# A pooled attention with a mixture of attention experts: five engine queues ordered anew, K pooling in wider matmuls, gates by counting, and another split of the last two output chunks

## The chip, the cores and the metric

The kernel runs on one core of one Trainium2 chip. The metric is device time in microseconds (us) of one execution, as the median of several runs. The profile is taken of one execution; its span runs from the first to the last instruction.

The engines have short names. PE is TensorE (matmuls; its weight loads are listed as PEld), DVE is VectorE, ACT is ScalarE, POOL is GpSimd, SP is SyncE. Each engine works through its own queue strictly in order. POOL also issues the input loads, SP the output stores.

## The reference

Two stages follow one another. Shapes: batch 8, heads 8, sequence 576, head size 64, so a token has 512 features; 4 experts with a head size of 64, of which each token uses 2.

```python
# stage 1: attention over keys and values averaged in groups of 8
k_p = k.reshape(B, H, S // 8, 8, D).mean(axis=3)      # 72 pooled keys
v_p = v.reshape(B, H, S // 8, 8, D).mean(axis=3)
attn = softmax(q @ k_p.T / sqrt(D))
x = (attn @ v_p)  # -> (B, S, H * D)
# stage 2: per token the two best of four experts, each a causal attention
logits = x @ w_gate
w = softmax over the top 2 logits of each token
for e in range(4):
    a = causal_softmax((x @ wq[e]) @ (x @ wk[e]).T / sqrt(Hd))
    ye = a @ (x @ wv[e]) @ wo[e]
    out += (e is in the token's top 2) * w * ye
```

## The kernel before, in words

Everything is unrolled. The work of a batch is cut into small steps, and the order of all steps of all eight batches is written out by hand in one long string, SEQ (lines 632 to 702). The loop below it reads the string token by token and emits the instructions of each step. A token is a name, arguments, a colon, the batch, and for matmul steps `@` and the PSUM bank; a trailing `d` puts a copy on DVE and not on ACT, a trailing `p` leaves a store to a later token. `tc.manual_schedule` keeps every engine's instructions in the order of the string, and only adds the waits that the data need. So the string fixes five queues at once, and where a token stands against one of another engine has no effect beyond those waits.

The steps of one batch, with their names in the string:

- Loads (`L`, line 112, on POOL): k and v in three thirds each, q in four quarters. They land in three rotating raw buffers each (NRAW = 3, line 55), cast to bf16 on the way. A load can start when the batch three before it has been read out.
- Pooling of k and v as matmuls with a pooling matrix: `PK` (line 265) and `PV` (line 284). For each third and each of two token parities, `PK` issues four matmuls on 32-wide strips of the array, 24 of 128 columns for a whole batch; batch 0 (LONG, line 59) is done in two halves of 64 columns. DVE turns the result (`kc`), a copy casts it (`kt`), another copies the pooled v (`vc`).
- DVE transposes q in two halves (`u0`, `u1`; line 293).
- Stage 1: scores `E`, exponential `e` on ACT, sums `D` and `d`, reciprocals `x`, weighted values `O`, and the scaled result `o` (DVE) into xT.
- Stage 2: values and gate logits `V`, `v`; query and key projections `P`, `p`; scores `S`, exponentials `s` (ACT, line 490), causal masks `a` (POOL, line 508), and the weighted values `B` with their scaling `bz`, `bg`, `b` (DVE, line 549).
- The gate `g0` to `g9` (line 397): an exponential on ACT, and eleven small DVE instructions that find the second largest of four logits by maxima and minima, compare, and normalize.
- The result is transposed on PE (`T`, copied by `t`) or by a DMA on SP (`F`, line 584). Then comes the output projection `Y` (line 592), its copy `y` (line 602) and the store `z` (line 617; `zs` on SP).

A batch's 576 tokens are four chunks of 128 and a tail of 64; the tails of two neighbouring batches share one chunk, number 4. In `Y`, the last chunk of all (batch 7, chunk 4) is computed in two halves of 256 columns in two banks. Tokens `ya` and `yb` copy the halves on ACT and DVE, and its two stores of 64 tokens go out on SP and ACT.

The exponential of the 64-token tile (`s` with tile number 3) is two ACT instructions, one for each expert of a pair:

```python
if ti == 3:
    for e in range(2):
        nc.scalar.activation(out=et[half(b), :, e, eo : eo + n], ...)
```

Of the kernel before, what the change touches and what calls it, by code (L numbers as in the profile page):

```python
# [16 lines left out]
ISEQ = mybir.AluOpType.is_equal  # L17
EXP = mybir.ActivationFunctionType.Exp
# [3 lines left out]
def kernel(  # L22
# [12 lines left out]
    nc = tc.nc  # L35
# [24 lines left out]
    HALF = TPP // 2  # L60

# [325 lines left out]
    def small(b, nm, *shape):  # L387
        if (b // 2, nm) not in at:
            at[b // 2, nm] = gtp.tile([128, NPC, *shape], FP32, name=nm, tag=nm)
        return at[b // 2, nm]  # L390
# [6 lines left out]
    def gate(b, step):  # L397
# [14 lines left out]
        elif step == 1:  # L412
            L2 = L.rearrange("p c (a b) -> p c a b", b=2)
            for nm, op in (("hi", MAXOP), ("lo", MINOP)):
                nc.vector.tensor_tensor(
                    out=tmp(nm, 2, 1), in0=L2[:, :, :, 0:1], in1=L2[:, :, :, 1:2], op=op
                )
        elif step == 2:
            for nm, src, op in (("s2", "hi", MINOP), ("s3", "lo", MAXOP)):
                nc.vector.tensor_tensor(  # L420
                    out=tmp(nm, 1), in0=got(src)[:, :, 0, :], in1=got(src)[:, :, 1, :], op=op
                )
        elif step == 3:
            nc.vector.tensor_tensor(
                out=tmp("m2", 1), in0=got("s2"), in1=got("s3"), op=MAXOP
            )
        elif step == 4:
            nc.vector.tensor_tensor(
                out=tmp("msk", E), in0=L, in1=got("m2").to_broadcast([128, n, E]), op=ISGE
            )  # L430
        elif step == 5:
            nc.vector.tensor_mul(out=tmp("W", E), in0=got("Ex"), in1=got("msk"))
        elif step == 6:
# [3 lines left out]
        elif step == 7:  # L437
# [4 lines left out]
        elif step == 8:  # L442
# [47 lines left out]
    def sb(b, bank, dve, ep, ti):  # L490
# [4 lines left out]
        if ti == 3:  # L495
            for e in range(2):
                nc.scalar.activation(
                    out=et[half(b), :, e, eo : eo + n],
                    in_=psum[half(b), bank + e, 0 : 2 * n].rearrange("p (a n) -> p a n", a=NEP),
                    func=EXP, scale=MOE_EXP_SCALE,  # L500
                )
# [90 lines left out]
    def Y(b, bank, c):  # L592
        p0 = 128 * place(b, c)
        last = (b, c) == (B - 1, 4)
# [7 lines left out]
    def y(b, bank, dve, c, half=None, later=False):  # L602
        ofin = at[b, "ofin", c] if (b, "ofin", c) in at else ofp.tile([128, DM], FP32, name="ofin", tag="ofin")
        if half is not None:
            cols = slice(256 * half, 256 * half + 256)
            copy(half == 1, ofin[:, cols], psum[:, bank ^ half, cols])
            at[b, "ofin", c] = ofin
            if (b, "half", c) not in at:
                at[b, "half", c] = True
                return  # L610
        else:
            copy(dve, ofin[:], psum[:, bank, :])
        at[b, "ofin", c] = ofin
        if not later:
            z(b, c, nc.sync)

    def z(b, c, queue):
        ofin = at[b, "ofin", c]
        if c == 4:
            for h in range(2):  # L620
                (nc.scalar if h and b == B - 1 else queue).dma_start(
                    out=out[b - 1 + h, MAIN:S, :], in_=ofin[64 * h : 64 * h + 64, :]
                )
# [12 lines left out]
        H1:0@0c H1:0@0c L_q1:1 H1:0@0c e21:0 e20:0 e11:0 D2:0@4 D0:0@5 L_q2:1 PV:0@6 d0:0 D1:0@7 vc:0d H1:0@0 x0:0  # L636
        c0:0d L_q3:1 d2:0 O00:0@6 d1:0 c1:0d O20:0@5 O01:0@4 o00:0 O10:0@2 x1:0 O11:0@3 o01:0 x2:0 X0:0@0 W2:0 o10:0
        X1:0 o11:0 X2:0 W3:0 c2:0d X3:0 c3:0d o20:0 P_k0:0@4 L_v0:1 h0:0 P_t0:0@5 p_k0:0d L_v1:1 P_k1:0@3 p_t0:0 L_v2:1
# [3 lines left out]
        d1:1 g1:0 E2:1@06 D0:1@2 vc:1d a03:0 x1:1 H1:0@3 L_v1:2 e20:1 g2:0 O11:1@3 e21:1 g3:0 O10:1@4 d0:1 o11:1 D2:1@5  # L642
        O01:1@6 L_v2:2 S10:0@0 x0:1 o10:1 S12:0@2 d2:1 s10:0 o01:1 S11:0@4 O00:1@7 g4:0 PK:2@6 s11:0 o00:1 L_k0:3
        O20:1@0 B01:0@1 kc:2 x2:1 B00:0@7 L_k1:3 g0:0 P_q1:1@4 o20:1 kt:2 bz00:0 bz01:0 s12:0 g5:0 L_k2:3 V2:1@0 g6:0
        g7:0 P_q0:1@6 g8:0 L_q0:3 v2:1 u1:2 p_q1:1 P_t0:1@0 a11:0 u0:2 p_q0:1 E1:2@24 L_q1:3 p_t0:1 g9:0 P_k0:1@6
        bg00:0 a10:0 e10:2 b00:0 bg01:0 L_q2:3 b01:0 V0:1@7 e11:2 p_k0:1d a12:0 E0:2@02 v0:1d B10:0@6 L_q3:3 W4:0 e01:2
        V4:1@4 bz10:0 B11:0@7 bg10:0 L_v0:3 b10:0 e00:2 PV:2@5 v4:1d D1:2@6 bz11:0 L_v1:3 P_k1:1@4 vc:2d d1:2 bg11:0
        b11:0 x1:2 E2:2@02 L_v2:3 D0:2@6 p_k1:1d e21:2 O11:2@7 O01:2@5 d0:2 O00:2@2 o11:2 O10:2@4 L_k0:4 e20:2 PK:3@3
        x0:2 o10:2 S03:1@0 S10:1@6 L_k1:4 s03:1 o01:2 s10:1 S01:1@0 o00:2 L_k2:4 V3:1@4 s01:1 kc:3 V1:1@5 L_q0:4 v3:1d
        S02:1@6 S11:1@2 v1:1 kt:3d S12:1@0 s02:1 L_q1:4 V2:2@4 u1:3 P_q1:2@5 a03:1 u0:3 s11:1 L_q2:4 P_q0:2@6 v2:2d  # L650
        s12:1 a02:1 p_q1:2d S00:1@2 L_q3:4 p_q0:2d g0:1 E0:3@04 s00:1 g1:1 L_v0:4 P_k0:2@6 g2:1 e00:3 g3:1 a12:1 g4:1
        P_k1:2@7 p_k0:2d e01:3 L_v1:4 E2:3@02 g5:1 B12:0@6 g6:1 L_v2:4 g7:1 e20:3 B02:0@4 g8:1 e21:3 bz12:0 T10:0@5
        g9:1 p_k1:2 a10:1 E1:3@02 bg12:0 t10:0d L_k0:5 b12:0 bz02:0 B12:1@5 bg02:0 e11:3 b02:0 PK:4@6 L_k1:5 bz12:1
        bg12:1 PV:3@4 b12:1 e10:3 kc:4 S00:2@2 L_k2:5 D1:3@5 vc:3d B01:1@6 s00:2 L_q0:5 kt:4d B02:1@7 T00:0@4 bz01:1
        V1:2@0 d1:3 bz02:1 L_q1:5 bg01:1 bg02:1 T02:0@1 t00:0d T01:0@2 D2:3@3 x1:3 b02:1 D0:3@5 a11:1 b01:1 O10:3@4
        d2:3 O00:3@7 t01:0d d0:3 L_q2:5 D2:2@6 v1:2d T11:0@3 V0:2@2 t02:0 o10:3 x0:3 a01:1 T12:0@5 V3:2@1 u0:4 L_q3:5
        t12:0 v0:2 O20:2@4 O01:3@5 v3:2 O11:3@0 a00:1 o00:3 t11:0 d2:2 L_v0:5 PV:4@1 o11:3 x2:2 x2:3 E0:4@26 o01:3 vc:4
        a00:2 Y3:0@0 L_v1:5 e01:4 o20:2 P_q1:3@5 y3:0dp e00:4 L_v2:5 T12:1@4 u1:4 B10:1@1 P_k1:3@0 p_q1:3 t12:1d bz10:1
        L_k0:6 bg10:1 E1:4@26 b10:1 p_k1:3 g1:2 P_t0:2@5 L_k1:6 e11:4 g2:2 V0:3@4 p_t0:2d Y2:0@0 e10:4 v0:3d Y1:0@5
        y2:0dp L_k2:6 V2:3@4 y1:0p g3:2 E2:4@26 O20:3@0 L_q0:6 v2:3d D1:4@1 e21:4 D0:4@5 o20:3 e20:4 PK:5@4 d1:4 L_q1:6  # L660
        u0:5 S02:2@2 d0:4 S10:2@6 V4:3@1 kc:5 s02:2 B11:1@5 kt:5d P_k0:3@4 v4:3 g4:2 bz11:1 a02:2 s10:2 bg11:1 b11:1
# [128 lines left out]
```

## Time and profile before

| what | value |
|---|---|
| median of 3 runs | 154.63 us (154.28 to 155.75) |
| span of the profiled execution | 152.5 us |
| granted PE clock, mean | 0.997 |
| data moved by DMA | 26.67 MB |
| input loads (queue of POOL) | 14.72 MB |
| DMA transposes on SP | 16 |

The time of the profiled execution itself isn't listed apart from the runs; its span is 2.1 us under their median. How to read the page: the busy shares say how long each engine had an instruction in work. The slices show the same over time, in tenths, for 40 equal slices of 3.8 us. The chain follows the work that ended last back to its causes. A group row gives the line, engine and operation, the shapes, the count, then busy time and mean length, then the idle time ahead of it and who ended it. A timeline row begins with the start and the length. In the windows, each engine's busy time in a stretch is followed by its number of instructions, and the row ends with the granted clock, the DMA share and the GB/s. An issue row of the DMA ends with the time from issue to landing.

### The profile page before, as it was taken

What the parts mean: (1) busy time and instruction counts of PE and PEld (TensorE: products, weight loads), DVE (VectorE), ACT (ScalarE), POOL (GpSimd) and SP (SyncE); (2) the same over time, 40 slices, a digit from 0 to 9 for tenths busy, and PEclk for the clock granted to TensorE, in tenths of its full rate; (3) what the DMA queues carried; (4) which work ended last, traced back from release to release, by engine and by line L of the source; (5) the groups of instructions that cost most, each with busy time, mean ns of one, the idle gap of its engine ahead of it and who ended that gap; (6) DMA issues with size and microseconds to landing.
All of it is one profiled execution on the core that took longest, in us unless ns stands there. A gap on an engine that the chain in (4) does not pass through costs nothing.

```text
span 152.5 us, 5419 instructions
## 1 busy us (share of the span) xinstructions
PE 140.5 (92%) x2101; PEld 78.8 (52%) x2122; DVE 125.9 (83%) x415; ACT 135.1 (89%) x247; POOL 89.5 (59%) x161
## 2 busy tenths in 40 slices
PE   6776998999999999999999999999999999999970
PEld 2323353465554465565546655856356667546640
DVE  1784846899899899899989999999897699888960
ACT  3359479999999999999999999999999899999860
POOL 6998588999688979958998171123300344442300
PEclk9999999999999999999999999999999999999998
DMA  4999999999999999999999931536528241389994
GB/s 126 237 186 181 181 179 178 180 180 181 179 188 180 179 181 182 178 180 182 169 173 176 181 34 39 211 84 208 176 92 325 83 121 25 66 282 306 333 340 134
DMA packets 68890, 26.67 MB, mean 175 GB/s; under 512 B 62720, under 2 KB 64000, under 8 KB 68864
## 3 DMA queue, kind: packets, MB, share of 16 engines
q0 software_dynamic: 57408, 14.72, 97.2%
q1 hardware_dynamic: 11088, 10.88, 22.2%
q10 hardware_dynamic: 368, 0.72, 1.5%
q8 instruction: 16, 0.26, 0.6%
q14 instruction: 10, 0.08, 0.2%
HBM read 30.42 MB, written 9.44 MB: 261 GB/s over the span
## 4 chain that ended last, share of the span: by engine, by line
PE 66%; DVE 11%; DMA 10%; POOL 4%; ACT 3%; issue 2%; DVEq 0%; POOLq 0%
PE psum L221 65%; DMA qraw<-in_q_dram 5%; DMA wst_q<-in_moe_wq_dram 4%; DVE xT L377 4%; ACT etb L503 2%; POOL kraw L126 2%; POOL vraw L126 2%; PE psum L230 1%; DVE qT L298 1%; DVE osc L562 1%; DVE oT L212 1%; POOL qraw L126 1%; DVE vp L212 1%; DVE ofin L212 1%; ACT eta L331 1%
## 5 line engine op out<-in xcount | busy, mean ns | idle before, releaser
L503 ACT ACTIVATE etb<-psum 128x1024 bf16<-128x1024 f32 x48 | 47.2, 1032 | 0.8 <-PE psum L221 0.4
L520 POOL TENSOR_SCALAR_AFFINE_SELECT etb<-etb 128x256 bf16<-128x256 bf16 x64 | 25.7, 412 | 37.2 <-ACT etb L503 36.0
L331 ACT ACTIVATE eta<-psum 96x1024 bf16<-96x1024 f32 (+1 forms) x48 | 36.0, 802 | 1.1 <-PE psum L221 0.4
L221 PEld LDWEIGHTS <-etb 128*128 128x128 bf16 x480 | 18.0, 97 | 6.3 <-issue 3.5
L126 POOL DMA_DIRECT2D qraw<-in_q_dram x30 | 19.7, 662 | 2.5 <-DVE gt L557 0.8
L377 DVE TENSOR_TENSOR xT<-psum,rza 128x512 bf16<-128x512 f32 x32 | 20.2, 681 | 1.0 <-ACT rza L354 0.5
L221 PE MATMUL psum<-wvg,xT 128*128 128x260 bf16 x144 | 20.8, 275 | 0.1
L126 POOL DMA_DIRECT2D kraw<-in_k_dram x25 | 19.0, 765 | 2.3 <-POOLq L774 0.8
L221 PE MATMUL psum<-vaug,etb 128*128 128x65 bf16 x480 | 20.2, 193 | 0.0
L126 POOL DMA_DIRECT2D vraw<-in_v_dram x24 | 18.8, 785 | 2.3 <-PE psum L221 1.4
L221 PE MATMUL psum<-xT,wqp 128*128 128x64 bf16 (+1 forms) x123 | 19.2, 282 | 0.5 <-issue 0.2
L221 PE MATMUL psum<-xT,wkp 128*128 128x64 bf16 (+1 forms) x121 | 18.8, 281 | 0.4
L221 PE MATMUL psum<-wop,oT 128*128 128x512 bf16 (+1 forms) x67 | 17.9, 373 | 0.5 <-DVE oT L212 0.3
L212 DVE CAST qk<-psum 128x512 bf16<-128x512 f32 (+1 forms) x23 | 15.0, 653 | 3.6 <-PE psum L221 3.6
L562 DVE TENSOR_TENSOR osc<-psum,gt 128x256 bf16<-128x256 f32 (+2 forms) x40 | 16.7, 421 | 1.0
L221 PE MATMUL psum<-qk 64*128 64x64 bf16 (+4 forms) x192 | 16.2, 277 | 0.6 <-DVE xT L377 0.2
L221 PEld LDWEIGHTS <-xT 128*128 128x128 bf16 x144 | 12.6, 97 | 6.9 <-issue 3.0
L212 ACT COPY ofin<-psum 128x512 f32<-128x512 f32 (+1 forms) x25 | 14.0, 587 | 1.1 <-PE psum L221 0.9
L298 DVE STREAM_TRANSPOSE qT<-qraw 128x576 f32<-128x576 f32 (+1 forms) x18 | 13.2, 750 | 1.0 <-DMA qraw<-in_q_dram 0.9
L221 PE MATMUL psum<-qT,kpT 32*128 32x64 bf16 (+1 forms) x256 | 12.5, 289 | 1.1 <-DVE qT L298 0.9
L221 PE MATMUL psum<-eta,vp 96*32 96x512 bf16 (+1 forms) x256 | 12.7, 288 | 0.5 <-DVE vp L212 0.5
L221 PEld LDWEIGHTS <-wqp 128*128 128x128 bf16 x128 | 8.4, 97 | 8.4 <-issue 2.3
(79 smaller groups left out, 214.4 us busy)
## 6 DMA issues: line engine op xcount, KB each, us to landing
out_dram<-ofin SPq DMA_DIRECT2D x32, 256.0 KB, 2.9
vraw<-in_v_dram POOLq DMA_DIRECT2D x24, 192.0 KB, 6.7
qraw<-in_q_dram POOLq DMA_DIRECT2D x30, 144.0 KB, 7.0
kraw<-in_k_dram POOLq DMA_DIRECT2D x21, 192.0 KB, 7.5
out_dram<-ofin SPq DMA_DIRECT2D x7, 128.0 KB, 2.4
xT<-in_q_dram ACTq DMA_DIRECT2D x2, 288.0 KB, 4.7
xT<-in_k_dram SPq DMA_DIRECT2D x2, 192.0 KB, 4.9
kraw<-in_k_dram POOLq DMA_DIRECT2D x4, 96.0 KB, 5.2
```

The source lines that it names most:

```text
L126: nc.gpsimd.dma_start(out=dst, in_=src)
L212: (nc.vector.tensor_copy if dve else nc.scalar.copy)(out=out, in_=in_)
L221: nc.tensor.matmul(out=out, lhsT=lhsT, rhs=rhs, start=start, stop=stop)
L230: nc.tensor.transpose(out=out[s], in_=in_[:, s], identity=ident[0:n, 0:n])
L298: nc.vector.transpose(out=dst.rearrange("p (a s n) -> p a n s", s=32, n=n)[:, :, own], in_=src.rearrange("p (a n d) -> p a n d", n=n, d=32 ...
L331: nc.scalar.activation(out=dst, in_=src, func=EXP, scale=ATT_EXP_SCALE)
L377: nc.vector.tensor_tensor(out=xT[:, 2 * got[0][0] + t : 2 * got[-1][0] + t + 1 : 2, m + got[0][1].start : m + got[0][1].stop], in0=psum[:, ...
L503: nc.scalar.activation(out=et[:, ep, :, eo : eo + n], in_=psum[:, bank : bank + 2, 0:n], func=EXP, scale=MOE_EXP_SCALE,)
L520: nc.gpsimd.affine_select(out=blk, in_=blk, pattern=[[0, 2], [1, 128]], compare_op=ISGE, fill=0.0, base=0, channel_multiplier=-1,)
L562: nc.vector.tensor_tensor(out=osc(b, ep)[:, own, :].rearrange("p c (e d) -> p e c d", e=2), in0=o[:, :, :, 0:HD], in1=gt.to_broadcast([128 ...
```

## The change

- **PK** of batches 1 to 7 takes all three thirds in one matmul: 8 matmuls of 384 columns in place of 24 of 128. Batch 0 stays.
- **The gate** compares each logit with the other three (one instruction, 64 or 80 elements for a group of 4 or 5 token chunks), sums the comparisons, and keeps the exponentials of the logits that fewer than two others exceed. Seven DVE instructions in place of eleven.
- **The 64-token exponential** is one ACT instruction in place of two.
- **The end**: in batch 7 it is chunk 3 that is computed and copied in halves (FINAL = 3). Chunk 4 is whole, copied by ACT (`y4:7p`), and its two stores are the tokens `z4:7` (ACT's queue) and `zs4:7` (SP's queue).
- **The order**: all tokens from behind batch 1's first scores are new: the order on PE, DVE, ACT, POOL and SP, the banks, and the engine of some copies. Of the copies, ACT gives DVE six projection casts (`p`), three `t`, one `kt` and one `y`, and takes two `v`. The loads are no longer sorted by batch: the last k third of batch 6 comes behind loads of batch 7, the last two v thirds of batch 5 behind loads of batch 6. Two stores of batch 0 stand on SP ahead of the first DMA transpose.

```diff
+    FINAL = 3
...
     def PK(b, bank, j=None):
...
-        for c in range(3):
+        for cs in [slice(c, c + 1) for c in range(3)] if b in LONG else [slice(0, 3)]:
             for t in range(2):
                 for i in range(4):
-                    mm(psum[32 * i : 32 * i + 32, bank, n * c : n * c + n], poolk[:, :],
-                       raw[:, c, pair(b, i)][:, own(j), t, :], start=(t == 0), stop=(t == 1))
+                    mm(psum[32 * i : 32 * i + 32, bank, n * cs.start : n * cs.stop], poolk[:, :],
+                       raw[:, cs, pair(b, i)][:, :, own(j), t, :], start=(t == 0), stop=(t == 1))
...
         elif step == 1:
+            nc.vector.tensor_tensor(
+                out=tmp("ahead", E, E), in0=L.unsqueeze(2).to_broadcast([128, n, E, E]),
+                in1=L.unsqueeze(3).to_broadcast([128, n, E, E]), op=ISGT,
+            )
         elif step == 2:
+            nc.vector.reduce_sum(out=tmp("c1", E), in_=got("ahead"), axis=mybir.AxisListType.X)
         elif step == 3:
+            nc.vector.scalar_tensor_tensor(
+                out=tmp("W", E), in0=got("c1"), scalar=1.5, in1=got("Ex"), op0=ISLT, op1=MULT,
+            )
...
         if ti == 3:
-            for e in range(2):
-                nc.scalar.activation(
-                    out=et[half(b), :, e, eo : eo + n],
-                    in_=psum[half(b), bank + e, 0 : 2 * n].rearrange("p (a n) -> p a n", a=NEP),
-                    func=EXP, scale=MOE_EXP_SCALE,
-                )
+            nc.scalar.activation(
+                out=et[half(b), :, :, eo : eo + n].rearrange("p a e n -> p e a n"),
+                in_=psum[half(b), bank : bank + 2, 0 : 2 * n].rearrange("p e (a n) -> p e a n", a=NEP),
+                func=EXP, scale=MOE_EXP_SCALE,
+            )
...
-        last = (b, c) == (B - 1, 4)
+        last = (b, c) == (B - 1, FINAL)
...
-            for h in range(2):
-                (nc.scalar if h and b == B - 1 else queue).dma_start(
-                    out=out[b - 1 + h, MAIN:S, :], in_=ofin[64 * h : 64 * h + 64, :]
-                )
+            for h in range(2) if b < B - 1 else [int(queue is nc.scalar)]:
+                queue.dma_start(out=out[b - 1 + h, MAIN:S, :], in_=ofin[64 * h : 64 * h + 64, :])
```

Three stretches of the string after the change, the loads of batches 5 to 7 and the end, the rest left out:

```
L_v0:5 ... a00:2 ... a01:1 ... L_v2:6 L_k2:6 L_q0:6 L_q3:6 L_v0:6 L_k1:7 L_k1:6 L_v1:5 L_q2:6 L_q1:6 L_v2:5 L_v1:6 a11:2 L_k0:6
...
p_k1:4d u0:6 E1:5@04 ... v0:4d ... p_q0:4d PV:5@6 ... PV:6@3 ... PK:6@0
...
Y2:7@7 t12:6 yb3:7d ya3:7 T12:7@5 y2:7p zs1:6 zs3:7 zs2:7 t12:7d Y4:7@4 y4:7p z4:7 zs4:7
```

More of the change, by code (lines that the diff above doesn't have):

```diff
@@ L436, in gate @@
             )
[L437 removed]
+        elif step == 5:
             nc.vector.scalar_tensor_tensor(
@@ L606, in y @@
             copy(half == 1, ofin[:, cols], psum[:, bank ^ half, cols])
[L607 to L610, printed above, removed]
         else:
             copy(dve, ofin[:], psum[:, bank, :])
-        at[b, "ofin", c] = ofin
-        if not later:
-            z(b, c, nc.sync)
+            if not later:
+                z(b, c, nc.sync)
     def z(b, c, queue):
```

149 lines of the change are left out of this document (67 added, 82 removed).

## The prediction

> **What bounds the kernel now.** I read the page from the top: busy shares, slices, the shares of the chain.
>
> ```profile
> span 152.5 us, 5419 instructions
> PE 140.5 (92%) x2101; PEld 78.8 (52%) x2122; DVE 125.9 (83%) x415; ACT 135.1 (89%) x247; POOL 89.5 (59%) x161
> ...
> PE   6776998999999999999999999999999999999970
> ...
> DMA  4999999999999999999999931536528241389994
> ...
> PE 66%; DVE 11%; DMA 10%; POOL 4%; ACT 3%; issue 2%; DVEq 0%; POOLq 0%
> ```
>
> TensorE is full from slice 8 to slice 38, and the chain lies on it for two thirds of the span. The DMA row has two full stretches: the loads, to about 88 us, and the last stores. Next come the windows. The first instruction the change moves stands on PE at 29.82 us and the last matmul ends at 148.1, so I asked for exactly that stretch, and for two parts of it.
>
> ```profile
> core 0: us, PE busy (x) PEld busy (x) DVE busy (x) ACT busy (x) POOL busy (x), PEclk, DMA share, GB/s
> 43.00:54.00 11.00, 10.61 (x155) 5.45 (x150) 10.22 (x33) 10.69 (x20) 9.87 (x18) 1.00 1.77 184
> 54.00:140.00 86.00, 85.15 (x1338) 50.19 (x1348) 78.32 (x261) 84.61 (x159) 42.28 (x84) 1.00 1.00 156
> 29.80:148.10 118.30, 116.27 (x1806) 68.18 (x1824) 106.98 (x358) 114.78 (x218) 64.53 (x121) 1.00 1.15 174
> ```
>
> Of 118.30 us PE is busy 116.27 and ACT 114.78: PE sets the time and ACT stands 1.5 us behind it, so work taken from ACT or DVE alone buys little. All the idle time of PE is 2.03 us. A busy PE can still be a slow one, so I compared its own blocks (the PE timeline; start, length, instruction).
>
> ```profile
> 29.82 0.62 PE L221 MATMUL psum<-eta,vp 96*32 96x512 bf16 x8
> ...
> 32.36 0.52 PE L221 MATMUL psum<-kraw,poolk 96*32 96x128 bf16 x24
> ...
> 36.92 1.04 PE L221 MATMUL psum<-xT,wkp 128*128 128x512 bf16 x4
> 37.80 0.61 PE L221 MATMUL psum<-wvg,xT 128*128 128x260 bf16 x4
> 38.34 0.63 PE L221 MATMUL psum<-qT,kpT 32*128 32x512 bf16 x8
> 38.90 0.36 PE L221 MATMUL psum<-vaug,etb 128*128 128x65 bf16 x6
> 39.10 0.61 PE L221 MATMUL psum<-wvg,xT 128*128 128x260 bf16 x4
> ...
> 42.02 0.40 PE L221 MATMUL psum<-eta,onesd 96*32 96x512 bf16 x4
> 42.25 1.04 PE L221 MATMUL psum<-eta,vp 96*32 96x512 bf16 x16
> 43.11 0.51 PE L221 MATMUL psum<-kraw,poolk 96*32 96x128 bf16 x24
> 43.55 0.45 PE L221 MATMUL psum<-qk 64*128 64x64 bf16 x6
> ```
>
> ```profile
> 53.89 0.52 PE L221 MATMUL psum<-kraw,poolk 96*32 96x128 bf16 x24
> ```
>
> ```profile
> 82.43 0.51 PE L221 MATMUL psum<-kraw,poolk 96*32 96x128 bf16 x24
> ```
>
> Start to start, four matmuls of 512 columns take 0.88 us (36.92 to 37.80), six of 65 take 0.20 (38.90 to 39.10), and four of 512 on 32-wide strips, which run side by side, 0.23 (42.02 to 42.25). All fit about 0.417 ns a column (a quarter of it on four strips) plus 8 ns a matmul. Laid end to end at that price from 29.8, the blocks put the K poolings PK of batches 2, 3, 4 and 6 at 31.6, 42.4, 51.8 and 80.0; measured are 32.36, 43.11, 53.89 and 82.43. PE thus loses 0.7 us by 32, 1.4 more between batch 3's PK and batch 4's, and only 0.3 in the next 28 us. So it really is PE's work that bounds, with one soft place at 43 to 54.
>
> **The change part by part.**
>
> PK of batches 1 to 7 goes from 24 matmuls of 128 columns to 8 of 384: 16 fewer each, the same columns. Old price: 43.11 to 43.55, 0.44. New: two rounds of four strips. The 512-column round of 0.23 scaled by 384/512 gives 2 x 0.17 = 0.35, a saving of 0.10; by the score block, eight of 512 in 0.56 (38.34 to 38.90), it is 0.42, a saving of 0.02. I take 0.10: like PK, that round writes strips and changes no bank between its matmuls. Batch 1's PK comes before 29.8 and waits for loads, so six count: 0.6 us, bounds 0.1 to 0.7.
>
> The Trainium skill, "TensorE: Matmul & The Clock Gate", section "Wait — 56ns, not 53.3ns?", has a floor of about 25 ns from start to start however few columns; by it 24 matmuls need 0.60 us and dropping 16 would give nearly 0.3 us a batch, 1.7 in all. The trace disagrees: 24 in 0.44 us is 18 ns each.
>
> The gate loses four instructions per batch (eleven become seven) and ACT's tail exponentials are merged, two into one.
>
> ```profile
> L212 DVE CAST qk<-psum 128x512 bf16<-128x512 f32 x20 | 13.8, 688 | 2.9 <-PE psum L221 2.9
> ...
> L212 ACT COPY ofin<-psum 128x512 f32<-128x512 f32 x24 | 13.6, 596 | 0.6 <-PE psum L221 0.4 <-ACT oT L212 0.2
> ...
> L212 ACT CAST qk<-psum 128x512 bf16<-128x512 f32 x10 | 5.8, 590 | 0.5 <-PE psum L221 0.5
> ...
> L331 ACT ACTIVATE eta<-psum 96x256 bf16<-96x256 f32 x16 | 5.3, 376 | 0.1
> ...
> L497 ACT ACTIVATE etb<-psum 64x128 bf16<-64x128 f32 x16 | 3.5, 271 | 0.1
> ...
> L428 DVE TENSOR_TENSOR msk<-L,m 128x20 f32<-128x20 f32 x4 | 0.9, 235 | 0.1
> ```
>
> Gate: seven small instructions at about 0.19 us become three, and the two new ones read 64 or 80 elements. Their price is not in the trace; it lies between the 20-element compare (0.235) and the 512-element cast (0.688), near the compare, so 0.25. About 0.65 us a batch, 5 us of DVE. Exponentials: 2 x 0.271 against one of 256 elements, 0.376: 1.3 us of ACT over eight batches.
>
> Copies change engine too. By the order of the changed kernel six projection casts (four of 512 columns, two of 256), three oT copies, a kpT cast and one ofin copy go from ACT to DVE, and two vaug/L pairs come back. That is about seven large copies net: -4 us for ACT at 0.59, +4.8 for DVE at 0.69. ACT ends 5 us lighter, DVE level. None of it is on PE, so I count it at nothing by itself; the cover is PE's 116.27 against DVE's 106.98, 9 us, which in the stretch 43 to 54 is only 10.61 against 10.22. It can only help by shortening PE's 2.03 us of waits: bounds 0 and 2.0. I take 0.4, because the soft place at 43 to 54 has DVE nearly as full as PE and new casts are added there.
>
> The new order moves the loads on POOL. Its rows here, with where they land:
>
> ```profile
> 71.62 0.77 POOL L126 DMA_DIRECT2D vraw<-in_v_dram  x1
> ...
> 75.32 2.30 POOL L126 DMA_DIRECT2D kraw<-in_k_dram  x3
> ```
>
> ```profile
> vraw<-in_v_dram POOLq DMA_DIRECT2D x1, 192.0 KB, 5.5
> ```
>
> ```profile
> kraw<-in_k_dram POOLq DMA_DIRECT2D x1, 192.0 KB, 5.0
> ```
>
> Loads share one queue that is full, so I ask which old load had the same number of bytes before it. Batch 6's last K third is now issued late: it takes the old place of batch 7's first K third, issued 75.32, landed 5.0 us later, 80.3. Its PK stands at 79.2 laid end to end, and with the loss of the old kernel at that point (2.4) at 81.6: the load is 1.3 us early. Batch 6's last q quarter has the place of the v third issued at 71.62 and landed at 77.1; its first transpose (u0:6, on DVE) has moved up from 87.6 to 75.2 laid end to end, 77.4 with a loss of 2.2. That is 0.3 us of room. Behind u0:6 on DVE stand the vaug and qk casts of batch 4, and PE waits for those. POOL's own waits for masks stay alike.
>
> SP changes more than it looks.
>
> ```profile
> 91.78 1.18 SPq L587 DMA_TRANSPOSE oT<-osc  x1
> ...
> 138.10 9.83 SPq L625 DMA_DIRECT2D out_dram<-ofin  x13
> 148.65 0.47 SPq L621 DMA_DIRECT2D out_dram<-ofin  x1
> ```
>
> ```profile
> 134.00:136.00 2.00, 1.95 (x13) 0.93 (x12) 2.00 (x4) 2.00 (x3) 1.24 (x4) 1.00 0.97 326
> ```
>
> Before, SP's first work after the K loads is a transpose at 91.78 with every store behind it. Now two stores of batch 0 stand ahead of all transposes; their outputs are ready about 65 us (63.2 laid end to end, plus 2), among the loads. At 326 GB/s 256 KB take 0.8 us, so the loads behind fall back by 0 (if they slip between) to 1.6 us; I take 0.5, nearer the lower end since the loads move only about 180 GB/s. Room of 1.3 and 0.3 covers it but for 0.2 us on DVE, which I count as nothing on PE.
>
> The Trainium skill, "DMA: Bandwidth & Descriptors", section "Queues, rings and completion order", says an engine takes turns between queues packet by packet. By it these stores do delay loads, up to the 1.6; no run here shows it yet.
>
> The end. Chunk 3 is now cut in halves, and the last tokens' copy is whole, on ACT.
>
> ```profile
> 148.04 0.37 ACT L212 COPY ofin<-psum 128x256 f32<-128x256 f32 x1 [0.48 <-PE psum L221]
> 148.16 0.42 DVE L212 COPY ofin<-psum 128x256 f32<-128x256 f32 x1 [0.74 <-PE psum L221]
> ```
>
> The whole copy takes 0.60 (the 128x512 ofin row) in place of 0.42: +0.2. The two stores already left on SP and ACT and still do: nothing. After its last transpose SP has 19 stores' worth in place of 20, the same queue: nothing, while the DMA stays as full as above.
>
> Sum: -0.6 -0.4 +0.2 = -0.8. The span goes from 152.5 to 151.7; the runs' median, 154.63, stands 2.1 above the span, so 153.8.
>
> **The rivals.**
>
> Faster, the waits go. With ACT 5 us lighter, all 2.03 us of PE's idle time vanishes: -0.6 -2.0 +0.2 = -2.4, 152.2; it passes 1% from 1.2 us recovered. For it: ACT's 114.78 of 118.30. Against it: from 54 to 140 PE already works 85.15 of 86.00.
>
> Faster, every matmul dropped is worth its 18 ns: 6 x 16 x 18 ns = 1.7 in place of 0.6, 152.7. This is the effect of the floor cited above. Against it: 384 columns on four strips need two rounds of 0.17 us whatever the count.
>
> Slower, late q. POOL takes its queue in order, and the loads stand between masks that wait for ACT; the old kernel lost 1.79 us at one of them.
>
> ```profile
> 69.22 0.76 POOL L520 TENSOR_SCALAR_AFFINE_SELECT etb<-etb 128x256 bf16<-128x256 bf16 x2 [1.79 <-ACT etb L503]
> ```
>
> If such a wait falls ahead of batch 6's q and the two stores cost their full 1.6, the q lands at 80.5 where u0:6 wants it at 77.4. DVE stands 3.1 us with PE's casts queued behind: -0.8 + 3.1 = +2.3, 156.9. It decides for slower from 2.4 us of lateness. For it: DMA full to slice 23. Against it: between batch 5's first v third and that q, POOL's new order has only two masks.
>
> No effect: the pooling saves only 0.02 a batch and the new order wins nothing: -0.1 -0 +0.2, 154.7.
>
> **How the numbers follow.** About 1%, 1.55 us, is what can be told from no change: below 153.1 is faster, above 156.2 slower. Forecast (153.8): 0.46. No effect (154.7): 0.14. Waits go (152.2): 0.22. Dropped matmuls (152.7): 0.03. Late q (156.9): 0.15. So faster 0.25, same 0.60, slower 0.15. The range 152.0 to 156.5 holds all cases but the last; the forecast's own is 153.0 to 155.0.
>
> **What would show it.** PK blocks start-to-next in 0.35 and not 0.42. PE idle between the first moved instruction and its last matmul near 1.6 us. ACT's busy time near 130, DVE's near 126. Two output stores at about 65 us. u0:6 without a wait of over 0.5 us on its load. Wrong would be: PE idle over 3 us, DVE waits on qraw at 65 to 80, or the last store issued later than 2 us behind the last matmul.

## The result, and the profile after

The changed kernel is slower by a little: 155.88 us (155.27 to 156.41 in 13 executions) against 154.46 (154.22 to 155.75, also 13), a ratio of 1.0078 with a 95% interval of 1.0056 to 1.0099. A second set on another occasion (11 executions) gave 155.62 against 154.56, and 1.0096 (1.0056 to 1.0135); a ratio is worked out over the single executions and need not be the quotient of the two medians.

The page of the changed kernel, the lines that answer to those shown of before:

```profile
span 154.6 us, 5155 instructions
PE 144.2 (93%) x2010; PEld 76.7 (50%) x2010; DVE 124.3 (80%) x390; ACT 132.1 (85%) x232; POOL 88.7 (57%) x161
...
PE   6887998999999999999999999999999999999960
...
PEclk9978999999999999999999999999999999999997
DMA  4999999999999999999999997537330379579993
...
PE 70%; ACT 10%; DVE 8%; issue 4%; DMA 4%; ACTq 0%; DVEq 0%
```

ACT lost 3.0 us, where 5 were forecast, and DVE 1.6, yet PE is busy for 3.7 us longer with fewer instructions. That is a trap twice over. The trace of before lacks records: 2101 matmuls stand beside 2122 weight loads, one load each, where the new page has 2010 of both. A trace of the old order with all its 2122 matmuls (experiment e7) has PE busy for 143.3 us. And the PEclk row has a 7 in its third slice. In a window of two us there the granted clock was 0.50, and the matmuls of 512 columns followed one another at 0.4 us and not at 0.2:

```profile
core 0: us, PE busy (x) PEld busy (x) DVE busy (x) ACT busy (x) POOL busy (x), PEclk, DMA share, GB/s
10.00:12.00 2.00, 2.00 (x9) 0.58 (x5) 1.85 (x9) 1.71 (x2) 2.00 (x4) 0.50 1.82 180
```

The trace puts this dip at 9.5 to 12.9 us, where nothing has changed yet. It makes batch 1's PV, the last block that both kernels have alike, start at 30.00 us instead of 28.25. So the two traces are compared from that block on. From its start to the end of the last matmul the old kernel takes 119.82 us (28.25 to 148.07) and the new one 119.45 (30.00 to 149.45): the reordered work itself is 0.37 us shorter. In the window that answers to the prediction's 29.80:148.10, PE stands idle for 0.94 us, where it seemed to be 2.03. The rows for it are those of the first trace of the changed kernel, of its second trace (experiment e16_again), and of e7, which has the old order on PE:

```profile
31.45:149.50 118.05, 117.11 (x1729) 66.01 (x1728) 105.58 (x335) 111.69 (x203) 63.23 (x120) 1.00 1.15 170
```

```profile
30.30:148.10 117.80, 115.81 (x1710) 65.89 (x1728) 104.72 (x334) 111.51 (x203) 64.02 (x122) 1.00 1.16 170
```

```profile
29.99:148.35 118.36, 117.39 (x1824) 68.16 (x1824) 107.51 (x357) 114.87 (x218) 64.77 (x121) 1.00 0.95 104
```

The second trace shows 1.99 us of idle time again, and e7 shows 0.97 in the old order. What differs is the records: 18 matmuls are missing in the window of before (1806 beside 1824 loads) and 18 in e16_again, and none in the other two. Each missing one of 512 columns leaves a gap of about 0.05 us that looks like a wait, 1 us over the 18. So PE's real idle time was near 1 us in both orders, and the order did not shorten it.

What got longer lies behind the last matmul: from there to the end of the span 4.44 us became 5.16. The second trace of the changed kernel, e16_again, has the clock full from the start. Its span is 153.9 and its last matmul ends at 148.07 us, to the hundredth where it ended before:

```profile
147.32 0.75 PE L224 MATMUL psum<-wop,oT 128*128 128x512 bf16 x2
```

All of 1.40 us, the difference of the two spans, comes after this line. That the two matmuls end together is in part chance: in e16_again batch 1's PV starts 0.54 us later, and the work from there on is 0.54 us shorter. The windows of the last microseconds, first before, then that second trace of the changed kernel (the last two columns are the DMA's busy share and GB/s):

```profile
149.00:150.00 1.00, 0.00 (x0) 0.00 (x0) 0.00 (x0) 0.00 (x0) 0.00 (x0) 1.00 0.59 188
150.00:151.00 1.00, 0.00 (x0) 0.00 (x0) 0.00 (x0) 0.00 (x0) 0.00 (x0) 1.00 0.74 207
151.00:152.00 1.00, 0.00 (x0) 0.00 (x0) 0.00 (x0) 0.00 (x0) 0.00 (x0) 0.75 0.00 0
```

```profile
149.00:150.00 1.00, 0.00 (x0) 0.00 (x0) 0.00 (x0) 0.00 (x0) 0.00 (x0) 1.00 1.01 379
150.00:151.00 1.00, 0.00 (x0) 0.00 (x0) 0.00 (x0) 0.00 (x0) 0.00 (x0) 1.00 1.04 299
151.00:152.00 1.00, 0.00 (x0) 0.00 (x0) 0.00 (x0) 0.00 (x0) 0.00 (x0) 0.85 0.50 174
```

No engine computes in these rows. Before, the stores had drained by 151; now the DMA is full until 151 and works into the next window. The traces' records of the end give three parts, measured from the end of the last matmul. SP's first DRAIN comes once SP has seen its stores land; POOL's DRAIN is one of the last instructions of all. "POOL records" counts the records of POOL in the trace, its waits included.

| kernel | last store issued | SP's DRAIN | SP's DRAIN to the end | POOL's DRAIN | POOL records |
|---|---|---|---|---|---|
| before | +0.59 | +3.59 | 0.85 | 0.106 | 215 |
| changed, first trace | +0.70 | +3.88 | 1.28 | 0.250 | 201 |
| changed, e16_again | +0.71 | +4.55 | 1.28 | 0.250 | 201 |

Against before, e16_again adds 0.12 for the issue, 0.84 for the landing and 0.43 for the end proper: 1.39.

### The profile page after: what moved, and what is told of

Same layout as the page of the kernel before. It is cut to its first block, busy times and chain, and to the rows that moved or that the text cites. A ratio compares the mean times of both kernels' runs of the same rounds, so it can differ in the third digit from the quotient of the medians.

```text
span 154.6 us, 5155 instructions
## 1 busy us (share of the span) xinstructions
PE 144.2 (93%) x2010; PEld 76.7 (50%) x2010; DVE 124.3 (80%) x390; ACT 132.1 (85%) x232; POOL 88.7 (57%) x161
## 4 chain that ended last, share of the span: by engine, by line
PE 70%; ACT 10%; DVE 8%; issue 4%; DMA 4%; ACTq 0%; DVEq 0%
PE psum L224 67%; DMA xT<-in_q_dram 4%; ACT eta L334 3%; ACT etb L495 3%; PE psum L212 2%; ACT rza L353 2%; PE psum L233 1%; DVE qT L301 1%; DVE xT L380 1%; ACT rza L357 1%; DVE qk L215 1%; DVE osc L554 1%; DVE kpT L215 1%; DVE gt L549 1%; DVE vp L215 0%
## 5 line engine op out<-in xcount | busy, mean ns | idle before, releaser
L495 ACT ACTIVATE etb<-psum 128x1024 bf16<-128x1024 f32 x48 | 46.7, 1033 | 0.6 <-PE psum L224 0.3
L512 POOL TENSOR_SCALAR_AFFINE_SELECT etb<-etb 128x256 bf16<-128x256 bf16 x64 | 24.8, 409 | 32.8 <-ACT etb L495 28.2
L215 DVE CAST qk<-psum 128x512 bf16<-128x512 f32 (+1 forms) x29 | 18.4, 636 | 3.2 <-PE psum L224 2.9
L224 PE MATMUL psum<-wop,oT 128*128 128x512 bf16 (+1 forms) x74 | 20.2, 374 | 0.0
L224 PE MATMUL psum<-xT,wqp 128*128 128x64 bf16 (+1 forms) x128 | 19.7, 286 | 0.0
L224 PE MATMUL psum<-xT,wkp 128*128 128x512 bf16 (+1 forms) x128 | 19.3, 286 | 0.2 <-DVE kf L281 0.2
L215 ACT COPY ofin<-psum 128x512 f32<-128x512 f32 (+1 forms) x24 | 13.3, 581 | 1.9 <-PE psum L224 1.1
L224 PE MATMUL psum<-qT,kpT 32*128 32x64 bf16 (+1 forms) x256 | 13.4, 297 | 0.6 <-ACT etb L495 0.3
L212 PE MATMUL psum<-warm 128*128 128x512 bf16 (+1 forms) x32 | 11.5, 508 | 2.2 <-DVE onesd L180 1.3
L215 DVE CAST vaug<-psum 128x256 bf16<-128x256 f32 x24 | 10.0, 420 | 4.2 <-PE psum L224 4.2
```

The source lines that it names most:

```text
L212: nc.tensor.matmul(out=psum[rows, bank, :], lhsT=warm[:, rows], rhs=warm[:], start=True, stop=True)
L215: (nc.vector.tensor_copy if dve else nc.scalar.copy)(out=out, in_=in_)
L224: nc.tensor.matmul(out=out, lhsT=lhsT, rhs=rhs, start=start, stop=stop)
L495: nc.scalar.activation(out=et[:, ep, :, eo : eo + n], in_=psum[:, bank : bank + 2, 0:n], func=EXP, scale=MOE_EXP_SCALE,)
L512: nc.gpsimd.affine_select(out=blk, in_=blk, pattern=[[0, 2], [1, 128]], compare_op=ISGE, fill=0.0, base=0, channel_multiplier=-1,)
```

## The experiments

They are told in the order in which they were made; the first theories looked at the wrong place. A ratio is always to the kernel before, measured on the same chip beside it (medians 154.40 to 154.56).

**The parts of the change, one by one.** Theory A held that the new order costs the time, B that a new form of an instruction does, C that the end does. e1 puts PK, the gate and the merged exponential into the old order; e2 takes the new order and end with the old forms.

```diff
 e1_edits (against before): functions PK, gate, small and sb as in the changed kernel
-    g3:0 ... g4:0 ... g9:0
+    g3:0 ... g4:0 ... g7:0
 e2_order (against the changed kernel): the same functions as before
-    g3:0 ... g4:0 ...
+    g3:0 g4:0 g5:0 ... g6:0 ...
```

> The old order and the old end, with the three shorter forms: K pooling in wide matmuls, gate by counting, one tail exponential. Theory A (the new order costs, by what it puts on the queues up to about 85 us): 153.9 to 154.5, no slower than the kernel before at 154.5, as the shorter forms only take work away. Rival B (one of the new forms is dearer than its old one, the pooling's 8 matmuls or the gate's sum): about 155.9, the whole loss. Rival C (the loss is the end: chunk 3 in halves, last tokens whole): as A, 153.9 to 154.5.

> The new order and the new end with the old forms of pooling, gate and tail exponential (each old gate step at the place of the new one). Theory A: at least as slow as the changed kernel, 155.9 to 156.8. Rival B: back at 154.5. Rival C: 155.9 to 156.8 too.

e1 took 154.78, ratio 1.0013 (0.9989 to 1.0037): the forms are worth nothing by themselves, and B falls. Its trace also prices the merged K pooling. Here are PK of batch 2 and of batch 7, before and then e1:

```profile
32.36 0.52 PE L221 MATMUL psum<-kraw,poolk 96*32 96x128 bf16 x24
101.06 0.55 PE L221 MATMUL psum<-kraw,poolk 96*32 96x128 bf16 x24
```

```profile
33.02 0.51 PE L223 MATMUL psum<-kraw,poolk 96*32 96x384 bf16 x8
101.64 0.54 PE L223 MATMUL psum<-kraw,poolk 96*32 96x384 bf16 x8
```

e1 starts this stretch 0.66 us late (a weight load that landed late, ahead of all that was edited) and is 0.58 late at its end. The stretch with five merged PKs, and the other shorter forms, gained 0.08 us, so at most about 0.02 for each PK.

e2 took 157.51, ratio 1.0189 (1.0159 to 1.0218). In the new order the old forms cost 1.6 us more than the new ones. Windows of e2 and of e16_again between the same blocks, first 28 to 46 and 46 to 55 us, then from batch 7's PV to the last matmul:

```profile
28.39:46.00 17.61, 16.85 (x275) 8.34 (x273) 15.30 (x47) 17.01 (x34) 15.57 (x26) 1.00 1.82 181
46.00:55.30 9.30, 8.47 (x123) 4.30 (x122) 8.81 (x28) 7.85 (x12) 8.88 (x16) 1.00 1.82 180
...
100.70:150.90 50.20, 48.14 (x670) 28.59 (x673) 42.45 (x163) 45.23 (x84) 12.90 (x35) 1.00 0.58 177
```

```profile
28.80:45.70 16.90, 16.41 (x255) 8.00 (x252) 14.48 (x43) 16.71 (x33) 15.54 (x26) 1.00 1.82 181
45.70:54.20 8.50, 8.39 (x112) 4.03 (x109) 7.93 (x24) 7.84 (x12) 8.21 (x15) 1.00 1.82 180
...
99.40:148.10 48.70, 47.90 (x654) 28.45 (x657) 41.33 (x147) 45.02 (x81) 12.82 (x35) 1.00 0.59 175
```

With the old forms the stretches are 0.7, 0.8 and 1.5 us longer. DVE's busy time grows by 0.8, 0.9 and 1.1 us in them, ACT's by 0.3, 0.0 and 0.2. Behind 100 us PE waits for DVE, of which e16_again has only 0.2 us:

```profile
PE psum L224 <- DVE osc L565: 0.9, 1, 0.9
PE psum L224 <- DVE ofin L215: 0.5, 1, 0.5
```

So the new order seems to have filled DVE with copies so far that the shorter gate is what makes room for them. The three old forms were only put back together, so that it is the gate is read from DVE's share and not shown by itself.

e3 and e4 separate the end: the changed kernel with the old end, and the old kernel with the new end.

```diff
 e3_oldend (against the changed kernel)
-    FINAL = 3
+    FINAL = 4
-    yb3:7d ya3:7 ... Y4:7@4 y4:7p z4:7 zs4:7
+    y3:7p ... Y4:7@4 ya4:7 yb4:7d z4:7 zs4:7
 e4_newend (against before): functions Y, y and z as in the changed kernel, FINAL = 3
-    y3:7p ... ya4:7 yb4:7d
+    yb3:7d ya3:7 ... y4:7p z4:7 zs4:7
```

> The changed kernel with the old end: chunk 3 whole, last tokens in halves on ACT and DVE, their stores on ACT and SP as before. Rival C: the profile of the changed kernel ends 5.15 us behind its last matmul, that of the kernel before 4.43, so 0.7 comes back: 155.2. Theory A: 155.7 to 155.9, the end is worth 0.2 at most.

> The kernel before with the new end alone: chunk 3 in halves, last tokens whole on ACT, stores on both queues. Rival C: 155.2, 0.7 slower. Theory A: 154.5 to 154.7.

e3 took 155.65, ratio 1.0070 (1.0046 to 1.0094), 0.2 below the changed kernel's first median and level with its second (155.62), so C does not explain it. e4 took 155.56, ratio 1.0065 (1.0045 to 1.0084): the same end costs 1.0 on the old order, where PE waits 0.51 us ahead of its last two matmuls and ACT 1.49 us ahead of its last copy. By the order, the second half of chunk 3 takes bank 0 there, which still holds another result; that reason was read, not tried. A was left.

**Without loads, and with few stores.** e5 and e6 leave the loads of batches 3 to 7 out of either kernel, e7 and e8 the stores of batches 0 to 6.

```diff
 e5_old_noloads (before), e6_new_noloads (changed): 50 load tokens taken out
-    L_k0:3 ... L_v2:7
 e7_old_fewstores (before), e8_new_fewstores (changed): 31 store tokens taken out
-    zs2:0 zs1:0 ... zs1:6
```

> The kernel before with the input loads of batches 3 to 7 left out (it computes those batches from the data of batches 0 to 2 that still stand in the buffers). It is the base for the same cut in the changed kernel. No wait for a load is left behind about 50 us. Theory A (the new order's loss lies in loads that come late, with two early stores among them): the old order has few load waits, so it gains only about 1 us, to about 153.5. Rival D (the loss lies in how the new order lines up PE, DVE and ACT, and at the end): the same 153.5 here; the two differ in the next run.

> The changed kernel with the input loads of batches 3 to 7 left out in the same way. Theory A: the gap of 1.4 us between the two kernels shrinks to the 0.7 us that the traces show behind the last matmul, or less, so at most 0.7 above the old order without loads. Rival D: the gap stays at 1.2 to 1.6 us, since no load takes part in it.

> The kernel before with the stores of batches 0 to 6 left out (31 store steps; only the last batch's rows and the last tokens are written). The base for the same cut in the changed kernel. Theory E (the new order has more bytes to store in its last 12 us, 4.3 MB against 3.4 MB, so its last stores land about 0.7 us later behind the last matmul): here the last stores land 0.3 to 0.5 us sooner than before, since the DMA was at 0.8 to 0.9 and not quite full: about 154.0. Rival F (the tail is the three serial copies on ACT): nothing, 154.5.

> The changed kernel with the same 31 store steps left out. Theory E: the stretch from the last matmul to the end falls from 5.15 to about 4.2 us, and the gap to the old order with few stores shrinks from 1.4 to about 0.7 us. Rival F: that stretch stays at 5.0 or more and the gap at 1.4 us, because the last store is issued late, behind ACT's copies. If the early stores at 67 us also hold up loads (Theory A), the gap falls below 0.7.

Without loads: 154.76 old, ratio 1.0019 (0.9994 to 1.0044), and 154.61 new, 1.0002 (0.9982 to 1.0023). The gap closed, as theory A said. With few stores: 154.77 old, 1.0026 (1.0007 to 1.0046), and 156.09 new, 1.0090 (1.0066 to 1.0114). The gap stayed at 1.3 us, so neither the two early stores nor the mass of the late ones makes it, which speaks against E; the tail of e8 was still 5.2 us, not 4.2.

e8's trace brought another suspect, G. Rows of DVE, then of POOL, at the same time:

```profile
49.51 1.33 DVE L423 SCALAR_TENSOR_TENSOR W<-c,Ex 128x20 f32<-128x20 f32 x1
```

```profile
49.66 1.49 POOL L512 TENSOR_SCALAR_AFFINE_SELECT etb<-etb 128x256 bf16<-128x256 bf16 x4
```

An instruction of 0.17 us took 1.33, until POOL's four masks were nearly done. In that trace the stretch from batch 3's PK to its PV took 9.3 us in place of 8.5. The Trainium skill, "SBUF — State Buffer", section "Who interferes with whom", says that a DVE instruction with two inputs in SBUF contends with a GpSimd instruction that reads SBUF, and that one of them then waits. The traces agree: in fourteen traces (before, changed, e1 to e12), of the gate's instructions with two inputs that ran beside a mask 65 of 203 took over 0.15 us longer than their median, of those with one input none of 41, and of the 483 that ran beside neither a mask nor the issue of a load none. Beside the issue of a load alone it was 17 of 249.

**Masks, the gate, and the order of the loads.** e9 moves that one gate step away from the masks, e10 puts the loads back by batch, e11 and e12 leave out the masks of batches 1 to 7 in either kernel.

```diff
 e9_gatemove (against the changed kernel)
-    a12:1 g3:1 L_v2:4 ... L_v0:4 g4:1
+    a12:1 L_v2:4 ... L_v0:4 g3:1 g4:1
 e10_sorted (against the changed kernel; the load slots stay, 21 of them hold another load; loads alone shown)
-    L_v0:5 ... L_v2:6 L_k2:6 L_q0:6 L_q3:6 L_v0:6 L_k1:7 L_k1:6 L_v1:5
+    L_v0:5 ... L_v1:5 L_v2:5 L_v2:6 L_k2:6 L_q0:6 L_q3:6 L_v0:6 L_k1:6
 e11_old_nomasks (before), e12_new_nomasks (changed): 49 mask tokens taken out
-    a11:1 ... a12:7
```

> The changed kernel with one instruction of DVE moved: the gate's product W of batches 0 and 1 (step g3 of batch 1) stands behind the casts of batch 2's values and keys, directly ahead of the next gate step, and no longer ahead of them. Theory G (where a gate instruction, which reads and writes SBUF only, meets masks on POOL, it is held until they end: 1.33 us in place of 0.17 at 49.5 us in one trace of the new order, with four masks on POOL from 49.66 to 51.15; the loads in POOL's queue are what pushes those masks together): the instruction no longer meets the four masks, and the executions that lose 1 us there get it back: median 155.2 to 155.5, with none above 156.0 but for those with a lower clock. Theory A in its plain form (loads land too late for q and K): nothing changes, 155.9.

> The changed kernel with its loads put back into the order of their batches: the same slots in POOL's queue, other loads in them (the last v thirds of batch 3, 4 and 5 and batch 6's k earlier, batch 7's first loads later). Theory A in its plain form: the interleaved loads are what comes late, so this gains 0.5 to 1.3 us: 154.6 to 155.4. Theory G: only which masks the loads stand between matters, and the slots are unchanged: 155.6 to 156.1.

> The kernel before with the causal masks of batches 1 to 7 left out (49 steps, nearly all of POOL's work beside loads). The base for the same cut in the new order. Theory G: the old order has its gate instructions lengthened by about 2.5 us in sum, and loses about 0.5 us of that on PE: 153.8 to 154.3. Theory A in its plain form: about 154.3 to 154.5, since loads are little affected.

> The changed kernel with the same 49 mask steps left out. Theory G: without masks there is nothing for DVE to be held by, and the loads are issued no later: the gap to the old order without masks falls from 1.4 us to 0.3 or less. Theory A in its plain form: the loads still come late by the place that they have among themselves, and the gap stays at 1.0 to 1.4 us. If both have a part, the gap lies between.

e9: 155.69, 1.0078 (1.0050 to 1.0105), no gain, so G is real in single executions but not what the median pays for. e10: 154.84, 1.0019 (0.9998 to 1.0040), a gain of 1.0 that A foresaw. e11: 154.30, 0.9990 (0.9975 to 1.0004); e12: 154.72, 1.0027 (1.0001 to 1.0054), a gap of 0.4. Yet in neither trace of the changed kernel, nor in those of e3, e8 and e9, did PE, DVE or ACT wait for a load between 30 and 90 us; DVE did so for 0.7 us in e12 and for 0.1 in e10, and both are faster kernels than those. So what did the order of the loads do?

**Half the order each, and the kernel again.** e13 and e14 sort only the early or the late loads, e15 joins what seemed to help, e16_again is the changed kernel itself.

```diff
 e13_sortearly, e14_sortlate (against the changed kernel): as e10, in the loads of batches 0 to 4, or of 5 to 7
 e15_both (against e3_oldend): all loads as in e10, and g3:1 as in e9
```

> The changed kernel with only the loads of batches 0 to 4 back in the order of their batches (the last v third of batch 2 and the three of batch 3 earlier, first k and q of batches 3 and 4 later); the loads of batches 5 to 7 stay interleaved. If the loss arises at 30 to 55 us (H1): about 155.0. If it arises at 55 to 85 us (H2): 155.6 to 156.0. If it is spread over both (H3): about 155.4.

> The changed kernel with only the loads of batches 5 to 7 back in the order of their batches. H1: 155.6 to 156.0. H2: about 155.0. H3: about 155.4.

> The changed kernel with all loads back in the order of their batches, the old end (chunk 3 whole, the last tokens in halves), and the gate's product W of batches 0 and 1 moved as in the run before. If the terms add (1.0 for the loads, 0.2 each for the end and the gate step): 154.5, level with the kernel before. If the end and the gate step are worth nothing beside sorted loads: 154.8.

> The changed kernel itself, beside the others on one chip: 155.5 to 156.0, and a trace in which the clock is full from the start, so that PV of batch 1 starts at 28.2 to 28.9 us and the last matmul ends at 148.0 to 148.8.

e13: 155.16, 1.0034 (1.0008 to 1.0059). e14: 155.18, 1.0043 (1.0016 to 1.0071). Each half gains nearly the same 0.45, in different places of the program, which does not look like a late load. e15: 155.03, 1.0008 (0.9978 to 1.0037), level with before by its interval, and no better than e10. e16_again gave the trace shown above, and with it the end of all traces could be set side by side:

| kernel | SP's DRAIN | SP's DRAIN to the end | POOL's DRAIN | POOL records |
|---|---|---|---|---|
| e3, e8, e9 (new order) | +3.93, +3.92, +4.20 | 1.28, 1.30, 1.28 | 0.250, 0.240, 0.250 | 201 |
| e2 (new order) | +4.00 | 1.22 | 0.159 | 202 |
| e13, e14 | +4.22, +4.07 | 0.84, 0.84 | 0.102 | 203 |
| e10, e15 | +4.01, +3.99 | 0.84, 0.85 | 0.102, 0.106 | 205 |
| e1 (old order) | +4.47 | 0.84 | 0.102 | 209 |
| e4, e7 (old order) | +3.69, +3.79 | 0.84 | 0.102 | 215 |
| e5, e11, e6, e12 | +3.59, +3.60, +4.48, +4.29 | 0.83 to 0.85 | 0.102 to 0.106 | 130 to 145 |

The end proper is longer by 0.4 us in every kernel with 201 or 202 POOL records and in no other. Sorting loads by batch changes which waits they need, and so adds two to four wait instructions to POOL's queue. The Trainium skill, "Runtime: NRT & Kernel Launch", section "Instruction fetch mechanics", says that an engine's instructions are fetched by DMA in blocks and that crossing a block's boundary is mostly hidden. The traces show such fetches as packets of kind "instruction". The DMA queues of e16_again from 151 us on, and behind them the answer for before:

```profile
q14 instruction: 2, 0.02, 0.6%
```

```profile
DMA packets 0, 0.00 MB, mean 0 GB/s; under 512 B 0, under 2 KB 0, under 8 KB 0
```

**Only the number of POOL's instructions.** e17 adds four instructions behind all of POOL's work, e18 takes the old kernel's count down to 202.

```diff
 e17_pool4 (against the changed kernel), behind the loop over the tokens
+        for _ in range(4):
+            nc.gpsimd.memset(warm[:, 0:1], 0.0)
 e18_oldfewmasks (against before): eight mask tokens taken out
-    a03:6 ... a00:7 ... a12:7
```

> The changed kernel with four small instructions (each sets one column of an unused tile to zero) at the end of POOL's queue, behind its last mask, when POOL has nothing more to do: 205 POOL records in place of 201. Theory I (the place of POOL's last instructions in its instruction stream makes the end longer; putting the loads back by batch gained by adding two to four waits to that stream): POOL's last DRAIN falls from 0.25 to about 0.10 us, the stretch from SP's last DRAIN to the end from 1.28 to 0.84, and the time by about 0.45, to 155.1 to 155.3. Theory A (the order of the loads itself): no change, 155.6 to 155.9, and the DRAIN stays at 0.25.

> The kernel before with the masks of batch 7 and one step of batch 6's left out (the scores above the diagonal then count in those batches), which takes POOL's records from 215 to 202. Theory I: POOL's last DRAIN grows from 0.106 to about 0.25 us, the stretch from SP's last DRAIN to the end from 0.85 to 1.28, and the time by about 0.45 to 154.9 or 155.0. Otherwise: leaving out masks changes nothing or gains up to 0.2, as with all masks left out: 154.3 to 154.5.

e17: 155.29, ratio 1.0051 (1.0032 to 1.0071), POOL's DRAIN 0.102 and the end 0.84. With four useless instructions the end proper is 0.44 us shorter, and the median 0.3 to 0.6 lower (the ratios 1.0078 and 1.0096 became 1.0051, with intervals that overlap). e18: 154.84, ratio 1.0027 (1.0001 to 1.0053), DRAIN 0.157 and the end 1.22: with less work the old kernel got 0.4 us slower. A fetch at the very end goes and comes with it. DMA from 152.8 us in e17, and from 151.6 us in e18:

```profile
DMA packets 0, 0.00 MB, mean 0 GB/s; under 512 B 0, under 2 KB 0, under 8 KB 0
```

```profile
q14 instruction: 1, 0.01, 0.3%
```

Theory I holds: the number of instructions on POOL decides over 0.4 us at the end. The records show where the time goes. Behind SP's DRAIN POOL has two semaphore instructions and then its own DRAIN; in the thirteen traces with the short end each starts 0.08 us after the one before. With 201 records the DRAIN comes 0.37 to 0.39 us after the second of them, in all five traces; with 202 the second comes 0.40 us after the first, in both. Either way it is POOL's 197th record that is late. With 203 records the 197th is the first semaphore instruction, which has to wait for the stores anyway, with more it lies further ahead, and with 130 to 145 there is none. So a pause of 0.3 us stands at a fixed place of POOL's queue, and the number of instructions decides whether the end has to sit through it; the rest is the longer DRAIN. That the place is a block boundary is argued from the page, not shown. The packet at the very end isn't what POOL waits for: in e16_again it starts at 153.89 us, and the late DRAIN ends at 153.43.

## Why the prediction was right or wrong

It forecast 153.8, a gain too small to tell from no change; measured were 155.88 and a loss clear of the noise, though inside the same 1%. That is above the forecast's own 153.0 to 155.0 and inside the wider range. The sum of -0.8 should have been +1.1 to +1.4.

- **PK, -0.6.** Wrong in size. The step that failed is "I take 0.10": blocks of eight matmuls start the next 0.44 us later (47.06 to 47.50 in the changed kernel), as the 24 did. It was 0.02 each or less, 0.1 in all, the end of the range taken from the score block. Nor does the fitted price (0.417 ns a column, 8 ns a matmul) fit this block in either form: it gives 0.51 us for the 24 matmuls and 0.38 for the 8. The floor of 25 ns a matmul that the prediction weighs (the Trainium skill, "TensorE: Matmul & The Clock Gate", section "Wait — 56ns, not 53.3ns?") would have given 1.7 us in e1 too; e1 gained nothing, so on these strips the trace again disagrees.

```profile
47.06 0.51 PE L224 MATMUL psum<-kraw,poolk 96*32 96x384 bf16 x8
47.50 0.61 PE L224 MATMUL psum<-qk 64*128 64x64 bf16 x8
```

- **The waits, -0.4.** Right in size by luck. The stretch is 0.37 us shorter in one trace and 0.54 in the other, of which 0.1 at most is PK. But it did not come out of PE's waits: "All the idle time of PE is 2.03 us" failed, since about half of that was missing records, which the row shown there tells by its 1806 matmuls beside 1824 loads. Idle time was near 1 us before (0.97 in e7) and after (0.94), so the sign "near 1.6" could not test the term, and the rival "the waits go" had 1 us to gain and not 2. What else made the stretch shorter was not found. ACT's busy time fell by 3.0 us, to 132.1, where 5 and 130 were forecast; DVE's 124.3 is near the forecast 126. The prices of the gate (0.20 to 0.24 us for the new instructions in the first trace, 0.25 forecast) and of the merged exponential (0.380 against 0.376) were right. And 9 us of cover on DVE was too generous: e2 shows that without the shorter forms the new order is 1.6 us slower still.
- **The end on the engines, +0.2.** The copy took 0.58 us, as forecast, but no time of a run bears the term out: e3, with the old end, is 0.2 below one median of the changed kernel and level with the other.
- **The two early stores and the two late loads, nothing.** Right. The stores went out at 67.71 us (66.45 in e16_again), u0:6 ran at 80.57 with no wait for its load, and e8 gained nothing from leaving those stores out.

```profile
67.71 0.86 SPq L611 DMA_DIRECT2D out_dram<-ofin  x2
```

```profile
80.57 0.77 DVE L301 STREAM_TRANSPOSE qT<-qraw 128x576 f32<-128x576 f32 x1
```

- **The last stores, nothing.** This step failed: "After its last transpose SP has 19 stores' worth in place of 20, the same queue: nothing". The count was right, but not what matters, which is how much is left when PE stops. By the packets of the traces the old kernel has 736 KB to move behind the last matmul, the changed one 922 and 1170. The prediction did not ask when that last transpose comes: SP issued it at 131.75 us before and at 134.60 in e16_again, so nearly the same stores start almost 3 us later; no run moves the transposes alone. SP's DRAIN came at +3.59 to +3.79 in six of seven traces of the old order, and at +3.88 to +4.55 in all thirteen of the new one: 0.45 us more in the middle, the later issue included. Bytes alone don't settle it: e8 had 768 KB and +3.92, e1 (old order) 772 KB and +4.47.
- **The end proper, not in the sum.** +0.43 by POOL's instruction count, shown by e17, e18 and the records of all twenty traces. The prediction counted POOL's work and its queue, but not its instructions.

None of the rivals names the cause. "No effect" (154.7) comes nearest, since it drops the pooling and the waits; "late q" has the sign, but its place, u0:6, shows no wait.

What stays open: -0.4 or -0.5, +0.45 and +0.43 make +0.3 to +0.5, and the medians differ by 1.1 to 1.4, so 0.6 us or more has no cause that a run shows. e16_again adds up to the whole difference, but with 0.84 for the landing and with batch 1's PV 0.54 us late (28.79 in place of 28.25), ahead of the new order. Such a delay isn't the new order's own: e1 and e5 start that block at 28.9 and 29.0, as their K weights landed after 8.6 in place of 7.0 us; in e16_again they landed after 7.1, and DVE still waited 1.26 us for batch 1's q, where it had waited 0.88; why was not found. Over the traces with a full clock that block starts at 28.14 to 28.99 in the old order (28.27 in the middle of seven) and at 28.11 to 28.93 in the new (28.52 in the middle of eleven). e10 against e17, with the same 205 POOL records, leaves up to 0.45 us that the order of the loads may still cost (their intervals overlap a little). e5 and e6 point the same way: with 136 and 137 POOL records the end is short in both, and without loads the new order is no slower at all. Neither shows the place, since PE, DVE and ACT wait for no load between 30 and 90 us in the changed kernel. And a half clock before 13 us, as in the first trace and in e17's (mean clocks 0.983 and 0.984), seems to fall more often on the changed kernel: 8 of its 24 executions had a mean clock below 0.987, against 6 of 145 of the kernel before. Why, no run shows; without these executions the medians are 155.62 and 154.48, 1.14 apart. Last, a trace is one execution, and those profiled lie up to 0.85 us off the median of their kernel, so a term of a few tenths that rests on one trace is unsure by as much.

## What to carry to other kernels

When PE is full, compare kernels between the last block that they share and the last matmul, and then the stretch behind it by itself; here the engines' work got shorter, and the part of the loss that was found sat where no engine computes. Compare the numbers of matmuls and of weight loads before believing PE's idle time: a missing record looks like a wait. Count the bytes still to be stored when the last matmul ends, and not the stores in the queue. If an edit of a few instructions moves the time by a constant 0.4 us and no wait shows it, add a few harmless instructions to the queue that ends last before believing any story about order.

## What the runs showed of the hardware

- The number of instructions on POOL alone lengthens the end by 0.4 us: 201 and 202 records do (1.22 to 1.30 us from SP's DRAIN), 203 to 215 and 130 to 145 don't (0.83 to 0.85). The late record is POOL's 197th in all seven traces that have the longer end.
- The clock can be granted at half for 3.4 us early in an execution; in the trace with it batch 1's PV started at 30.00 us, 1.75 later than before.
- On 32-wide strips, merging 24 matmuls of 128 columns into 8 of 384 left the time to the next block at 0.44 us.
- A DVE instruction of 0.17 us with two inputs in SBUF took 1.33 us beside four masks on POOL, so it was held through more than one of them.
